# Products with v ahead of a burst's last transposed score, and both bursts of a unit in the order transposed, score, score, transposed

## The chip, the core and the metric

The kernel runs on one core of a Trainium2 chip. The metric is the device time of one execution in microseconds; the time before is the median of three runs. The engines are TensorE (PE; its weight loads are the rows PEld), VectorE (DVE), ScalarE (ACT), GpSimd (POOL) and SyncE (SP), which issues the DMAs. Everything here about the hardware is read from the traces of this kernel.

## What is computed

A block with attention and an MLP side by side, on 2048 rows of 512 features: 32 heads of 16 features, and a hidden layer of 1792.

```python
def _A_ref(x, wqkv, wo):
    qkv = (x @ wqkv).reshape(B, S, 3, H, Dh).transpose(2, 0, 3, 1, 4)
    q, k, v = qkv[0], qkv[1], qkv[2]
    scores = jnp.einsum("bhqd,bhkd->bhqk", q, k) * (Dh ** -0.5)
    p = _softmax(scores, axis=-1)
    o = jnp.einsum("bhqk,bhkd->bhqd", p, v)
    return o.transpose(0, 2, 1, 3).reshape(B, S, D) @ wo

def _B_ref(x, w1, b1, w2, b2):
    h = _gelu(jnp.einsum("bsd,df->bsf", x, w1) + b1)
    return jnp.einsum("bsf,fd->bsd", h, w2) + b2

xn = _layernorm(x)
return x + _A_ref(xn, A_wqkv, A_wo) + _B_ref(xn, B_w1, B_b1, B_w2, B_b2)
```

## The kernel before

**Work.** A prologue (to some 99 us) normalises x, splits it and the first weights into two f16 parts each, and computes the first scores. Then a single stream of *units* carries everything else: attention is cut into 512 units, each with four heads, 512 queries and 128 keys, and the *dense* products (the rest of the projections, both layers of the MLP, the output projection) are put between, some with each unit. A short tail finishes the output projection.

**What a unit does.** For each of its four heads there are three kinds of product:

- *S*, a score (queries by keys, `s_half`, tile pS). VectorE takes its row maximum (L363). It belongs to a unit 19 ahead (`LEAD`), so that the maximum is known in time.
- *T*, a transposed score (keys by queries, `e_half`, tile pT). ScalarE takes its exponential into a tile pe (L410).
- *V*, the product of pe with v (`v_half`, tile pV), in f32. It uses exponentials of one or two units earlier. A row of ones in v gives the sums of the softmax as well.

**Row halves.** Scores contract over 64 rows or fewer. So every product uses one half of the rows of TensorE's array, lower (rows 0 to 63) or upper (64 to 127), and two products in different halves can run side by side. Each product is four instructions, one for each group of 32 columns (`tiled`, L195). A head with an even number works in the lower half, an odd one in the upper half. `v_half` takes two heads' worth of work in a half: keys 0 to 63 with a = 0, keys 64 to 127 with a = 1; its f32 operands make two passes of four instructions.

**A burst.** `unit` (L745) makes two *bursts*, a = 0 and a = 1. Each gives TensorE two T, two S, one V and three or four dense products, in this order of the program:

- a = 0: T1 (upper), S0 (lower), S1 (upper), T0 (lower), then V in the upper half, then dense products in the lower half.
- a = 1: S2 (lower), T3 (upper), S3 (upper), T2 (lower), then V in the lower half, then dense products in the upper half.

So each half has V in one burst of a unit and the dense products in the other. The number of dense products is the group's `pace` (FAST is four in each burst, SLOW three, MEAN three and four by turns). A dense group of 12 or 42 products for each half adds up in one PSUM bank, then ScalarE or VectorE evicts it (`one_more`, L670, issues that after a burst's scores).

**The fence.** V of one burst and V of the next write the same accumulator from different halves, and so do the dense products. They must not overlap. `leave` (L178) lets the last V and the last dense product of a burst raise a semaphore, if the accumulation goes on; a dense group that is finished raises none there. `enter` (L187) sets a goal, and the first product afterwards waits until all these have signalled. In the trace this wait stands on V's first weight load. Everything behind it in TensorE's queue waits too.

**Banks.** S takes turns in three PSUM banks, T in three, a dense group holds one. `hold` (L112) gives a new dense group the bank that T used longest ago; the finished group's bank goes to T (`Group.end`, L550). For the first burst of the 16 units of an accumulation (`new`), V comes after the dense products.

**Who sets the order.** The order on every engine is the order of the program (`manual_schedule`, L840). In the stream of units it is written by hand in `unit`; a planner (`Plan`) orders the prologue alone.

Of the kernel before, what the change touches and what calls it, by code (L numbers as in the profile page):

```python
# [54 lines left out]
def layer_kernel(ctx: ExitStack, tc: tile.TileContext, x, wqkv, wo, w1, b1, w2, b2, out):  # L55
# [51 lines left out]
    def banks(tag):  # L107
        k = free_banks[tag].pop(0)
        free_banks[tag].append(k)
        return bank_tile(k, tag)  # L110

    def hold(tag, other):  # L112
        k = free_banks[tag if free_banks[tag] else other].pop(0)
        return bank_tile(k, tag), (k, other)
# [44 lines left out]
    def given(engine, ns):  # L159
        backlog[engine] += ns  # L160
# [6 lines left out]
    def product(user, *args, **kw):  # L167

        p = nc.tensor.matmul(*args, **kw)  # L169
        if user is None:  # L170
            return
        if goal[0] is not None:
            p._wait_ge(turns, counted[0])
            tc.declare_fence(p.ins, group=goal[0])
            goal[0] = None
        newest[user] = p

    def leave(user, goes_on):  # L178

        p = newest.pop(user, None)  # L180
        if p is not None and goes_on:
            p.then_inc(turns, 1)
            tc.no_tile_sem_insts.add(p.ins.name)
            counted[0] += 1
            left.append(p)

    def enter():  # L187

        if left:
            goal[0] = f"turn{counted[0]}"  # L190
            for p in left:
                tc.add_to_no_dep_group(goal[0], p.ins)
            left.clear()

    def tiled(user, dst, lhs, rhs, start, stop):  # L195

        for j in range(0, P, 32):
            product(user, dst[j:j + 32], lhs[:, j:j + 32], rhs, start=start, stop=stop)
# [11 lines left out]
    def fetch_scale(m):  # L210

        scale_of[m] = nc.scalar.alloc_register(f"sexp{m}")
        nc.scalar.reg_load(scale_of[m], sexp[0:1, m:m + 1].bitcast(I32))
# [152 lines left out]
    def s_half(u, n):  # L366

        s = banks("S")
        s_mm(u, n, s)
        s_max(u, n, s)  # L370

    def s_end(u):

        t, i = divmod(u, 16)
        if i < 15:
            return
        g, qb = divmod(t, NQB)
        mneg = mnegs[t % 2]
        nc.vector.tensor_reduce(mneg[:, :16], mt_of[t].rearrange("p h t k -> p (h t) k"), axis=AX.X, op=ALU.max, negate=True)
        given("dve", 220)  # L380

        def store():

            pt = banks("T")
            for a in range(2):
                nc.tensor.matmul(pt[32 * a:32 * a + 32, :64], mneg[64 * a:64 * a + 64, :],
                                 ident[64 * a:64 * a + 64, 64 * a:64 * a + 64], start=True, stop=True)
            mhl = work.tile([64, 2, 64], F16, name="mhl", bufs=2)
            nc.vector.tensor_scalar_mul(mhl[:, 0], pt[:64, :64], 1.0 / MROW)
            nc.vector.scalar_tensor_tensor(mhl[:, 1], pt[:64, :64], 1.0 / MROW, mhl[:, 0], op0=ALU.mult, op1=ALU.subtract)  # L390
            given("dve", 300)
            for a in range(2):
                nc.sync.dma_start(m_d[t, :, :, 64 * a:64 * a + 64], mhl[32 * a:32 * a + 16])
            for h in range(4):
                m_rows(t, h)

        stores[t] = store

    def e_half(u, n):

        p, a = divmod(n, 2)
        t, kt = divmod(u, 16)
        g, qb = divmod(t, NQB)
        st = banks("T")
        r = slice(64 * a, 64 * a + 64)
        k0 = (kt % 4) * P
        tiled(None, st, kst[g % 2][kt // 4][r, p, k0:k0 + P], qst[g % 2][qb][r, p, :], True, True)
        pe = work.tile([P, QB], F32, name="pe", bufs=12)
        ptiles[u, n] = pe
        nc.scalar.activation(pe, st, AF.Exp, scale=scale_of[g // 2])  # L410
        given("act", 520)

    def v_half(u, a):

        t, kt = divmod(u, 16)
        g, qb = divmod(t, NQB)
        if kt == 0 and a == 0:
            pv_of[t] = hold("V", "S")
        pv = pv_of[t][0]
        r = slice(64 * a, 64 * a + 64)  # L420
        for h in (2, 3, 0, 1):
            c = (4 * g + h) * VW
            product("V", pv[32 * h:32 * h + 32, :], vv[r, kt, c:c + 32], ptiles[u, h][r],
                    start=(kt == 0 and a == 0), stop=(kt == 15 and a == 1))
# [77 lines left out]
    NU = NG * NQB * 16  # L502
# [155 lines left out]
    def ended(at_once=True):  # L658

        if cur[0] is not None and cur[0].over():  # L660
            done, cur[0] = cur[0], None
            ends.append(done.end)
            if at_once:
                settle()
# [5 lines left out]
    def one_more():  # L670

        if ends:
            ends.pop(0)()
        elif extras:
            extras.pop(0)()
# [10 lines left out]
    def dense(gen, side):  # L686

        f = group(gen)
        for _ in range(0 if f is None else f.pace[pos[0] % 2]):
            if not f.usable(side):  # L690
                return
            f.product(side)
# [25 lines left out]
    def spare(gen, side):  # L718

        if extra[0] is None and not spent[0]:  # L720
            f = next(gen, 0)
            spent[0] = f == 0
            extra[0] = Halves(f) if f else None
        if extra[0] is not None:
            extra[0].product(side)
            if extra[0].at == extra[0].n:
                extra[0] = None
# [17 lines left out]
    def unit(gen):  # L745


        u = pos[0]
        e = u - LEAD
        if e > 0 and e % (2 * NQB * 16) == 0 and e < NU:  # L750
            fetch_scale(e // (2 * NQB * 16))
        pos[0] += 1
        for a in range(2):
            for kind, b in ((1, 1), (0, 0), (0, 1), (1, 0)) if a == 0 else ((0, 2), (1, 3), (0, 3), (1, 2)):
                if kind and 0 <= e < NU:
                    e_half(e, b)
                elif not kind and u < NU:
                    s_half(u, b)
                elif not kind and u > NU:
                    spare(gen, b % 2)  # L760
            if e >= 0:
                one_more()
                enter()

                w, r = (e - 2, 1) if a == 0 else (e - 1, 0)
                live = 0 <= w < NU
                new = r == 0 and w % 16 == 0
                if live and not new:
                    v_half(w, r)
                dense(gen, 1 - r)  # L770
                if live and new:
                    v_half(w, r)

                for user, goes_on in (("V", live and not (r == 1 and w % 16 == 15)),
                                      ("D", cur[0] is not None and not cur[0].over())):
                    leave(user, goes_on)
                for k in backlog:
                    backlog[k] = max(0, backlog[k] - HALF)
                if live and r == 1:
                    v_end(w)  # L780
                ended(False)

            if a == 0 and u % 16 == 0 and u // 16 - 1 in stores:
                stores.pop(u // 16 - 1)()
        if u < NU:
            s_end(u)
        tick()
# [9 lines left out]
    with ExitStack() as st1:  # L797
# [252 lines left out]
        for w in (1, 0):  # L1050
# [5 lines left out]
            else:  # L1056
                a = add("POOL", 800, lambda wf=wf, i1=i1: nc.gpsimd.tensor_scalar(tl[wf], tl[wf], i1, 0.0, op0=ALU.mult, op1=ALU.add), [h])
                w_ready[w] = add("POOL", 1100, lambda wf=wf, hi=hi, lo=lo: nc.gpsimd.tensor_tensor(lo, tl[wf], hi, op=ALU.subtract), [a], free=[wf])
        a = add("DVE", 90, lambda: nc.vector.tensor_tensor(sexp[:, 0:1], fac0[:, 0:1], fac0[:, 1:2], op=ALU.mult), [chain])
        a = add("DVE", 90, lambda: nc.vector.tensor_scalar_mul(sexp[:, 0:1], sexp[:, 0:1], DH ** -0.5), [a])  # L1060
# [5 lines left out]
        a = add("DVE", 90, lambda: nc.vector.tensor_tensor(amv[:, 2:3], amv[:, 0:1], amv[:, 1:2], op=ALU.max), v_sum)  # L1066
# [3 lines left out]
        for i in range(2):  # L1070
# [6 lines left out]
            else:  # L1077
                b = add("POOL", 1240, lambda key=key: nc.gpsimd.tensor_scalar(
                    tl[key], tl[key], inv_v[:, 0:1], 0.0, op0=ALU.mult, op1=ALU.add), [h])
# [30 lines left out]
        a = add("DVE", 220, maxima, m_last)  # L1110
# [3 lines left out]
        def turn_m():  # L1114
            tl[mkey] = sb_tile(mkey)
            for k in range(2):
# [3 lines left out]
        a = add("PE", 300, turn_m, [a], take=[mkey])  # L1120
        a = add("DVE", 160, lambda: nc.vector.tensor_scalar_mul(mhl[:, 0], tl[mkey][:64, :64], 1.0 / MROW), [a])
        a = add("DVE", 160, lambda: nc.vector.scalar_tensor_tensor(mhl[:, 1], tl[mkey][:64, :64], 1.0 / MROW, mhl[:, 0],
                                                                   op0=ALU.mult, op1=ALU.subtract), [a], free=[mkey])
# [371 lines left out]
```

## Time and profile before

| | us |
|---|---|
| median of three runs | 1475.2 (1474.68 to 1475.99) |
| the profiled execution | 1476.9 |
| its span, first to last instruction | 1475.1 |
| TensorE busy, at least one row half | 1458.9 |
| VectorE busy | 1356.4 |
| ScalarE busy | 1260.5 |
| GpSimd busy | 662.4 |
| granted TensorE clock | 0.997 |

A row of the timeline is: start, length, engine, line of the kernel, operation, tile written and tiles read, shape, number of instructions run together, and in brackets the idle time before it with what ended it. Lengths of rows with several instructions run from the first start to the last end. The end of a matmul is modelled, and two matmuls in one half overlap at their ends, so the time that a product holds its half is read from start to start. A row with `x8` of a 4-instruction product holds two products. TensorE's products nearly all stand under L169, the helper that records them, so one goes by tiles: pT, pS, pV, pD.

### The profile page before, as it was taken

Reading aid. Unit: us, or ns where it says so; the run is one execution under the profiler, and the core shown is the slowest. Engines: PE = TensorE matmul, PEld = TensorE weight load, DVE = VectorE, ACT = ScalarE, POOL = GpSimd, SP = SyncE. Lnnn points to the kernel's source line nnn. Section 1 sums busy time; section 2 is a strip of 40 time slices with the busy share of each in tenths; the row PEclk is TensorE's granted clock in tenths of the full one; section 3 lists DMA queues with packets and bytes.
Section 4 is the critical chain, followed back from the end, with each engine's and each line's share of the span. In section 5 each row is a group of like instructions: output and inputs, shape, how many; then the busy total and the mean of one; then the engine's idle time right before and its main releaser. Section 6 shows DMA issues by size and latency. Waiting matters only on the chain.

```text
span 1475.1 us, 88125 instructions
## 1 busy us (share of the span) xinstructions
PE 1458.9 (99%) x40158; PEld 817.6 (55%) x40158; DVE 1356.4 (92%) x2305; ACT 1260.5 (85%) x2366; POOL 662.4 (45%) x672
## 2 busy tenths in 40 slices
PE   8999999999999999999999999999999999999998
PEld 4445555565555555555555555555555555555554
DVE  7889999999999999999999999999999999999933
ACT  5868888888999888899988889998889999888884
POOL 3201847563778401287830138783115777121100
PEclk9999999999999999999999999999999999999999
DMA  7732455545224210221113111121112110221432
GB/s 214 225 117 69 151 186 172 169 159 159 78 59 128 66 34 25 70 61 41 45 43 87 30 37 44 51 76 44 44 37 76 55 37 21 57 55 31 142 94 96
DMA packets 112623, 124.83 MB, mean 85 GB/s; under 512 B 22908, under 2 KB 84220, under 8 KB 112248
## 3 DMA queue, kind: packets, MB, share of 16 engines
q1 hardware_dynamic: 112248, 119.18, 27.0%
q8 instruction: 314, 5.14, 1.4%
q14 instruction: 61, 0.50, 0.1%
HBM read 81.66 MB, written 37.34 MB: 81 GB/s over the span
## 4 chain that ended last, share of the span: by engine, by line
PE 95%; ACT 2%; DVE 1%; DMA 1%; issue 0%; SPq 0%; DVEq 0%; ACTq 0%
PE pV L169 29%; PE pD L169 25%; PE pT L169 19%; PE pS L169 19%; PE pT L992 2%; DMA wq<-in_A_wqkv_dram 1%; PE pD L992 1%; DVE mt L363 1%; ACT pe L410 0%; DVE ac L1370 0%; DMA m_d<-mhl 0%; PE pT L962 0%; ACT xs L945 0%; ACT hh L1312 0%; PE pS L1158 0%
## 5 line engine op out<-in xcount | busy, mean ns | idle before, releaser
L363 DVE TENSOR_REDUCE mt<-pS 128x1 f32<-128x512 f32 x2029 | 1278.9, 684 | 54.9 <-PE pS L169 27.0
L410 ACT ACTIVATE pe<-pT 128x512 f32<-128x512 f32 x2048 | 1111.4, 599 | 168.1 <-PE pS L169 79.8
L169 PE MATMUL pV<-pe,vv 64*32 64x512 f32 x8192 | 1074.3, 594 | 0.1
L169 PE MATMUL pT<-qst,kst 64*32 64x512 f16 x8192 | 707.4, 377 | 2.0 <-issue 1.3
L169 PE MATMUL pS<-kst,qst 62*32 62x512 f16 x8116 | 611.1, 378 | 1.2 <-DVE mt L363 1.2
L169 PEld LDWEIGHTS <-qst 62*32 62x32 f16 x8192 | 286.0, 92 | 228.9 <-issue 55.3
L169 PE MATMUL pD<-xb,wc 64*32 64x512 f16 x5376 | 362.1, 377 | 0.0
L169 PEld LDWEIGHTS <-kst 64*32 64x32 f16 x8192 | 276.1, 91 | 154.7 <-issue 62.1
L169 PE MATMUL pD<-w_s,g 64*32 64x512 f16 x5376 | 358.0, 377 | 0.0
L169 PEld LDWEIGHTS pV<-pe,vv 64*32 64x32 f32 x8192 | 182.3, 105 | 89.2 <-PE pV L169 4.2
L169 PE MATMUL pD<-xt,wqk_h 64*32 64x512 f16 x2400 | 158.7, 378 | 0.1
L169 PEld LDWEIGHTS <-wc 64*32 64x32 f16 x5376 | 117.2, 91 | 41.0 <-issue 0.7
L169 PEld LDWEIGHTS <-g 64*32 64x32 f16 x5376 | 114.5, 92 | 39.7 <-issue 0.3
L1337 POOL TENSOR_TENSOR xa<-xa,yt 128x512 f32<-128x512 f32 x16 | 20.5, 1280 | 226.8 <-ACT yt L1335 226.8
L466 POOL TENSOR_TENSOR osb<-osb,rb 128x512 f32<-128x512 f32 x31 | 39.8, 1284 | 165.3 <-DMA rb<-den_d 154.2
L1289 POOL TENSOR_TENSOR t<-hh 128x512 f32<-128x512 f32 x56 | 58.2, 1039 | 84.0 <-ACT hh L1312 83.1
L1291 POOL TENSOR_TENSOR t<-t,hh 128x512 f32<-128x512 f32 x56 | 71.8, 1282 | 4.7
L1284 POOL TENSOR_TENSOR t<-t,hh 128x512 f32<-128x512 f32 x56 | 71.7, 1281 | 4.7
L1286 POOL TENSOR_TENSOR g<-t,g 128x512 f16<-128x512 f32 x56 | 65.2, 1164 | 4.7
L1283 POOL TENSOR_SCALAR t<-t,gs 128x512 f32<-128x512 f32 x56 | 38.8, 693 | 63.3 <-ACT t L1278 63.3
L169 PEld LDWEIGHTS <-wqk_h 64*32 64x32 f16 x2400 | 54.4, 92 | 20.5 <-issue 2.3
L169 PE MATMUL pD<-wo_s,oc 64*32 64x512 f16 x828 | 54.5, 378 | 0.0
(160 smaller groups left out, 873.1 us busy)
## 6 DMA issues: line engine op xcount, KB each, us to landing
wc<-w_d SPq DMA_DIRECT2D x56, 256.0 KB
qk_d<-stg SPq DMA_DIRECT2D x32, 256.0 KB
rb<-den_d SPq DMA_DIRECT2D x124, 64.0 KB
wch<-in_B_w_dram SPq DMA_DIRECT2D x14, 512.0 KB
wch<-in_B_w_dram SPq DMA_DIRECT2D x28, 256.0 KB
w_d<-wsp SPq DMA_DIRECT2D x28, 256.0 KB
kst<-qk_d SPq DMA_DIRECT2D x64, 96.0 KB
qst<-qk_d SPq DMA_DIRECT2D x64, 96.0 KB
```

The lines of the kernel that those rows point to most:

```text
L169: p = nc.tensor.matmul(*args, **kw)
L363: nc.vector.reduce_max(mt_of[t][:, n, qt, kb:kb + 1], s, axis=AX.X)
L410: nc.scalar.activation(pe, st, AF.Exp, scale=scale_of[g // 2])
L466: pooled((1280, lambda: nc.gpsimd.tensor_tensor(osb, osb, rb, op=ALU.mult)), (620, lambda: nc.gpsimd.tensor_scalar(ot[:, 0], osb, 1.0, 0.0 ...
L992: nc.tensor.matmul(tl[key], lhs, rhs, start=c + n == 0, stop=(c, n) == (NC - 1, 2))
L1283: pooled((690, lambda: nc.gpsimd.tensor_scalar(t1, t1, 1.0, gs[:, 1:2], op0=ALU.add, op1=ALU.mult)), (1280, lambda: nc.gpsimd.tensor_tenso ...
L1284: (1280, lambda: nc.gpsimd.tensor_tensor(t1, t1, hh, op=ALU.mult)),
L1286: (1160, lambda: nc.gpsimd.tensor_tensor(g[:, 1, f, :], t1, g[:, 0, f, :], op=ALU.subtract)),
L1289: pooled((1040, lambda: nc.gpsimd.tensor_tensor(t1, hh, hh, op=ALU.mult)), (620, lambda: nc.gpsimd.tensor_scalar(t1, t1, 1.0, 1.0 / GELU_A ...
L1291: (1280, lambda: nc.gpsimd.tensor_tensor(t1, t1, hh, op=ALU.mult)),
L1337: add = lambda: nc.gpsimd.tensor_tensor(xa, xa, yt, op=ALU.add)
```

## The change

The fence and V move ahead of the last of the burst's four T and S products, when V goes on with an accumulation (`early`). In the program the burst is then T, S, S, fence, V, T, dense. In the burst a = 1 the four products are put in another order: T2 (lower), S3 (upper), S2 (lower), T3 (upper), where it was S2, T3, S3, T2. So T0 (a = 0) and T3 (a = 1) come behind V. Where V begins an accumulation, and at the very end, the place of V and of the fence stays. The eviction of a dense group (`one_more`) is still issued after all four products.

```diff
         for a in range(2):
-            for kind, b in ((1, 1), (0, 0), (0, 1), (1, 0)) if a == 0 else ((0, 2), (1, 3), (0, 3), (1, 2)):
+            w, r = (e - 2, 1) if a == 0 else (e - 1, 0)
+            live = 0 <= w < NU
+            new = r == 0 and w % 16 == 0
+            early, placed = live and not new and e < NU, 0
+            for kind, b in ((1, 1), (0, 0), (0, 1), (1, 0)) if a == 0 else ((1, 2), (0, 3), (0, 2), (1, 3)):
                 if kind and 0 <= e < NU:
+                    if placed == 3 and early:
+                        enter()
+                        v_half(w, r)
                     e_half(e, b)
                 elif not kind and u < NU:
                     s_half(u, b)
                 elif not kind and u > NU:
                     spare(gen, b % 2)
+                placed += 1
             if e >= 0:
                 one_more()
-                enter()
-
-                w, r = (e - 2, 1) if a == 0 else (e - 1, 0)
-                live = 0 <= w < NU
-                new = r == 0 and w % 16 == 0
-                if live and not new:
+                if not early:
+                    enter()
+                if live and not new and not early:
                     v_half(w, r)
                 dense(gen, 1 - r)
                 if live and new:
```

In the diff `kind` is 1 for T and 0 for S, and `b` is the head.

## The prediction

> **What bounds the kernel now.** I read the page first, then the instructions that touch the accumulator pV, then the groups of TensorE, then stretches of the timeline.
>
> ```profile
> span 1475.1 us, 88125 instructions
> PE 1458.9 (99%) x40158; PEld 817.6 (55%) x40158; DVE 1356.4 (92%) x2305; ACT 1260.5 (85%) x2366; POOL 662.4 (45%) x672
> ...
> PE 95%; ACT 2%; DVE 1%; DMA 1%; issue 0%; SPq 0%; DVEq 0%; ACTq 0%
> ```
>
> ```profile
> L169 PEld LDWEIGHTS pV<-pe,vv x8192: 102/104/110, 99.2 to 1460.7; 64*32 64x32 f32 x200
> ```
>
> TensorE carries 95% of the chain of waits, but a busy share of 99% doesn't say whether both row halves of its array are busy. The bursts with products with v run from 99.2 to 1460.7 us: 1361.5 us for 512 units, 2.66 us a unit of two bursts, 92% of the span. The change acts only there. How much dense work goes into them:
>
> ```profile
> L169 PE MATMUL pD<-xb,wc 64*32 64x512 f16 x5376 | 362.1, 377 | 0.0
> L169 PE MATMUL pD<-w_s,g 64*32 64x512 f16 x5376 | 358.0, 377 | 0.0
> L169 PE MATMUL pD<-xt,wqk_h 64*32 64x512 f16 x2400 | 158.7, 378 | 0.1
> L169 PE MATMUL pD<-wo_s,oc 64*32 64x512 f16 x828 | 54.5, 378 | 0.0
> ...
> L169 PE MATMUL pD<-wvh,xt 64*32 64x512 f16 x480 | 31.5, 377 | 0.0
> ...
> L169 PE MATMUL pD<-wo_s,xb 64*32 64x512 f16 x336 | 22.6, 378 | 0.0
> ```
>
> Together 14,796 tiles, four to a product: 14796 / 4 / 1024 = 3.61 products a burst. So I treat 39% of the units as having three dense products a burst and 61% as having four. First the timeline of TensorE in a stretch with three (start, length, number of tiles):
>
> ```profile
> 463.27 0.62 PE L169 MATMUL pV<-pe,vv 64*32 64x512 f32 x4
> 463.30 0.61 PE L169 MATMUL pD<-xb,wc 64*32 64x512 f16 x8
> 463.71 0.61 PE L169 MATMUL pV<-pe,vv 64*32 64x512 f32 x4
> 463.73 0.39 PE L169 MATMUL pD<-xb,wc 64*32 64x512 f16 x4
> 463.95 0.39 PE L169 MATMUL pT<-qst,kst 64*32 64x512 f16 x4
> 464.14 0.42 PE L169 MATMUL pS<-kst,qst 62*32 62x512 f16 x8
> 464.36 0.40 PE L169 MATMUL pT<-qst,kst 64*32 64x512 f16 x4
> 464.53 0.63 PE L169 MATMUL pV<-pe,vv 64*32 64x512 f32 x4
> 464.58 0.61 PE L169 MATMUL pD<-xb,wc 64*32 64x512 f16 x8
> ```
>
> This is a burst with V in the lower half (463.27), followed by one with V in the upper half (464.53). An f16 product holds its half for 0.22 us (dense at 463.73, T1 behind it in the same half at 463.95). V comes in two passes 0.44 us apart and holds its half for 0.87: from 463.27 to S0 at 464.14. The lower half then runs S0 at 464.14, T0 at 464.36, dense at 464.58: no hole. The upper half runs T1 at 463.95, S1 0.22 behind it, and V could follow at about 464.38 but starts at 464.53.
>
> **What V waits for.** V's first weight load carries the fence of L187: the last V and the last dense product of the burst before must have signalled. The second pass of 463.71 ended at 463.71 + 0.61 = 464.32, the dense product at 463.73 + 0.39 = 464.12. V starts 0.21 after the later of the two. Three bursts on, a dense group had ended, so the fence waited for V alone:
>
> ```profile
> 465.82 0.62 PE L169 MATMUL pV<-pe,vv 64*32 64x512 f32 x4
> ...
> 466.26 0.61 PE L169 MATMUL pV<-pe,vv 64*32 64x512 f32 x4
> ...
> 466.91 0.40 PE L169 MATMUL pT<-qst,kst 64*32 64x512 f16 x4
> 466.96 0.63 PE L169 MATMUL pV<-pe,vv 64*32 64x512 f32 x4
> 467.13 0.39 PE L169 MATMUL pD<-xb,wc 64*32 64x512 f16 x4
> ```
>
> There V starts 0.09 after the end of the second pass (466.87), 0.12 sooner, although T0 stood just as long before (0.65 after the second pass in both). So the fence waited for the signal of a dense product that had ended 0.2 us before V: TensorE's signals seem to leave in the order of the program, each behind those ahead of it. ScalarE shows the same:
>
> ```profile
> 1197.66 0.61 PE L169 MATMUL pV<-pe,vv 64*32 64x512 f32 x4
> 1197.72 0.39 PE L169 MATMUL pT<-qst,kst 64*32 64x512 f16 x4
> ```
>
> ```profile
> 1198.61 0.60 ACT L410 ACTIVATE pe<-pT 128x512 f32<-128x512 f32 x1 [0.55 <-PE pS L169]
> ```
>
> T ended at 1198.11, V's second pass, ahead of it in the program, at 1198.27; the exponential of T starts at 1198.61 after 0.55 us of idle time.
>
> The Trainium skill (TensorE: Matmul & The Clock Gate, section The mechanism) says that matmuls both start and end strictly in the order of the program. The trace agrees on the ends, by the two waits just read. On the starts it does not: the dense products of 463.30 stand behind V's second pass in the program and start 0.41 us ahead of it.
>
> Now the stretch with four dense products:
>
> ```profile
> 471.19 0.59 PE L169 MATMUL pV<-pe,vv 64*32 64x512 f32 x1
> ...
> 471.62 0.59 PE L169 MATMUL pV<-pe,vv 64*32 64x512 f32 x2
> ...
> 472.49 0.62 PE L169 MATMUL pV<-pe,vv 64*32 64x512 f32 x4
> ...
> 473.82 0.59 PE L169 MATMUL pV<-pe,vv 64*32 64x512 f32 x1
> ```
>
> ```profile
> 472.47 0.13 PEld L169 LDWEIGHTS pV<-pe,vv 64*32 64x32 f32 x5
> ```
>
> The unit takes 473.82 - 471.19 = 2.63. A half's own work is V 0.87 + eight products (S, T, four dense, T, S) x 0.22 = 2.63: packed full. The fence opens at 472.47, 0.85 after the second pass, when S0 and T0 have just covered it. With three dense products the half's work is 2.41, but the unit takes 465.82 - 463.27 = 2.55, set by the fence in each burst. By shares: 0.39 x 2.55 + 0.61 x 2.63 = 2.60; the measured 2.66 leaves 0.06 a unit, 31 us in all, for other waits.
>
> **The change, part by part.**
>
> (1) The transposed score that was third or fourth in the burst (T0, or T3 in the other burst) now stands behind V's waiting weight load. Behind the load also stand the dense products and the next burst, as before; ScalarE waits for this T, and the group's eviction waits for the dense products. T was what filled the half while the fence was shut. Now that half has V's 0.87 and one S, is free at 1.09 after V's start, and waits for the fence.
>
> (2) When does it open? Second pass 0.44 after V's start, then 0.82 (463.71 to 464.53) with three dense products or 0.85 with four. New in it is T's own signal, which now lies between V's and the dense product's. The trace doesn't show that place. Bounds: 0, and the 0.12 that the signal of three dense products costs; I take 0.06, since T has fewer instructions than these. Then 0.05 for handing V over (V 464.53 to dense 464.58). T starts 0.44 + 0.82 + 0.06 + 0.05 = 1.37 after V's start with three, 1.40 with four.
>
> (3) A unit of one half then is that start plus T, the dense products, T and S: 1.37 + 6 x 0.22 = 2.69 with three, 1.40 + 7 x 0.22 = 2.94 with four. By shares 2.84; times 512 it is 1454 us, against 1361.5 now. The 0.06 of part (2) bounds it to 1423 and 1485.
>
> (4) The T moved behind V signals only after V's second pass. Its exponential follows V's start by 0.44 + 0.61 + some 0.15 of signals, about 1.2, and takes 0.6 (row above), so its bank is free about 1.8 after V's start. Three banks in turn cover that. When a dense group ends, though, the new one takes the oldest T bank, and the second T of the next burst gets the bank of its forerunner and waits from about 1.4 to 1.8. There are some 115 groups (5376 / 96 = 56 of the first dense layer, 16 of the second, the rest projections): at most 115 x 0.4 = 46 us, at least 0. With the 31 us of other waits that may stay or be swallowed by the new holes, this term lies between 0 and 77; I take 20, nearer the low end because a half that idles 0.3 us a unit absorbs much.
>
> (5) The new order in the second burst (T2, S3, S2, T3) leaves each half with the same products. It shifts a score or a T by one product, 0.22 us at most either way a unit. VectorE and ScalarE cover it:
>
> ```profile
> 857.77 1.27 DVE L363 TENSOR_REDUCE mt<-pS 128x1 f32<-128x512 f32 x2
> ```
>
> ```profile
> L363 DVE TENSOR_REDUCE mt<-pS 128x1 f32<-128x512 f32 x2029 | 1278.9, 684 | 54.9 <-PE pS L169 27.0
> L410 ACT ACTIVATE pe<-pT 128x512 f32<-128x512 f32 x2048 | 1111.4, 599 | 168.1 <-PE pS L169 79.8
> ```
>
> Two maxima back to back are 1.27 - 0.68 = 0.59 apart, 2.36 for a unit's four; that leaves 0.5 of 2.84. If VectorE were the bound, the 0.22 would cost up to 113 us. I count 0. No DMA is moved, and nothing passes SP's or POOL's queue.
>
> (6) V itself may start earlier than T0 let it (464.38 against 464.53); that gives nothing while the fence opens later than both.
>
> Sum: 1454 + 20 - 1361 = +113 us. The profiled execution took 1476.9 us, span 1475.1, and the runs' median is 1475.2; the sum on the execution gives 1590, on the median **1588**.
>
> **The rivals.**
>
> A. Only the cover is lost: T's signal costs nothing and the new holes swallow all other waits. For it: holes of 0.3 us a unit. Against it: signals that queue behind one another at 464.53. 1423 - 1361 = +62: 1537.
>
> B. Faster. V is held not by signals but by its place behind T0; ahead of T0 it starts when its half is free, and T0 still fills the other half. For it: V starts 0.17 after T0 (464.36 to 464.53) with its half free since 464.38. Against it: at 466.91 the same T0 is followed by V in 0.05. The gain would be 0.15 a burst in the 39% with three dense products, 400 x 0.15 = 60 us at most; VectorE's 2.36 a unit leaves room for it. I take 35: 1440. It decides if T0 starts within 0.7 of V's second pass, as it does now.
>
> C. No difference: VectorE sets the pace (92% busy) and TensorE's new holes fall into its waits. Against it: VectorE needs 2.36 of 2.66. 1475.
>
> D. T0 must wait until V's second pass has started, 0.44 later. Against it: the dense products at 463.30. 0.44 x 512 = 225 on top: 1813. That is what the Trainium skill's rule on starts (same section) would make of it.
>
> **How the numbers follow.** Forecast 0.61 (its own range 1545 to 1645), A 0.17, B 0.13, C 0.08, D 0.01. A measurement of this kernel can tell about 0.2%, 3 us, from no change. C gives 0.04 to the same, 0.03 to slower and 0.01 to faster. Slower is 0.61 + 0.17 + 0.01 + 0.03 = 0.82, faster 0.14, same 0.04. The range goes from C, 1474, up to 1650, the forecast with three quarters of the waits in (4) and T's signal at 0.1; B, D and what little of the others lies beyond are left out, under 2 in 10.
>
> **What would show it.** Right: the starts of V in a stretch with four dense products lie 1.4 to 1.5 apart instead of 1.31; the T behind V starts about 0.05 after the fence opens, some 0.9 after the second pass, with its half idle before it; ScalarE's wait for pT grows, VectorE's share falls to about 86%. Wrong: T0 starting 0.65 after the second pass as now, or V's spacing unchanged with three dense products; then the fence is not what holds the queue, and B or C is left.

## The result and the profile after

| | before | after |
|---|---|---|
| median of the runs, us | 1474.9 | 1631.5 |
| ratio to before | | 1.1057 (95% interval 1.1043 to 1.1072) |
| span of the profiled execution, us | 1475.1 | 1629.0 |
| stream of V, first to last weight load, us | 1361.5 | 1515.5 |

The change costs 157 us, and 154 of them lie in the stream of units. The page of the changed kernel (busy time and share of each engine, the rows of VectorE's maxima and ScalarE's exponentials with their idle time ahead), and the row of V's weight loads with their first and last start:

```profile
span 1629.0 us, 88631 instructions
...
PE 1609.9 (99%) x40158; PEld 914.1 (56%) x40158; DVE 1384.4 (85%) x2305; ACT 1273.9 (78%) x2366; POOL 662.0 (41%) x672
...
L363 DVE TENSOR_REDUCE mt<-pS 128x1 f32<-128x512 f32 x2029 | 1304.3, 685 | 171.9 <-PE pT L169 108.7
L410 ACT ACTIVATE pe<-pT 128x512 f32<-128x512 f32 x2048 | 1124.2, 597 | 308.6 <-PE pT L169 262.6
```

```profile
L169 PEld LDWEIGHTS pV<-pe,vv x8192: 102/106/110, 99.1 to 1614.6; 64*32 64x32 f32 x200
```

TensorE's own row still says 99%: one half idles while the other works, and the busy share can't show it. VectorE and ScalarE show it. Idle time ahead of the maxima rose from 54.9 to 171.9 us, ahead of the exponentials from 168.1 to 308.6, and nearly all the new waits are for pT. The same stretch as before, with three dense products a burst, on TensorE's timeline:

```profile
789.43 0.62 PE L169 MATMUL pV<-pe,vv 64*32 64x512 f32 x4
789.45 0.40 PE L169 MATMUL pT<-qst,kst 64*32 64x512 f16 x4
789.67 0.39 PE L169 MATMUL pD<-xb,wc 64*32 64x512 f16 x4
789.87 0.60 PE L169 MATMUL pV<-pe,vv 64*32 64x512 f32 x3
...
790.30 0.40 PE L169 MATMUL pS<-kst,qst 62*32 62x512 f16 x4
790.32 0.39 PE L169 MATMUL pT<-qst,kst 64*32 64x512 f16 x4
790.53 0.39 PE L169 MATMUL pS<-kst,qst 62*32 62x512 f16 x4
790.76 0.62 PE L169 MATMUL pV<-pe,vv 64*32 64x512 f32 x4
790.78 0.40 PE L169 MATMUL pT<-qst,kst 64*32 64x512 f16 x4
791.01 0.39 PE L169 MATMUL pD<-xb,wc 64*32 64x512 f16 x4
...
792.10 0.62 PE L169 MATMUL pV<-pe,vv 64*32 64x512 f32 x4
```

```profile
790.75 0.13 PEld L169 LDWEIGHTS pV<-pe,vv 64*32 64x32 f32 x5 [0.16 <-PE pD L169]
```

The upper half has V at 789.43 and 789.87 and one product at 790.30. It is free at 790.52 and then stands empty until T at 790.78. T came 0.03 after V's weight load, 0.91 after the second pass, 1.35 after V's start. In the kernel before, T0 ran 0.65 after the second pass, in that hole. The trace also records when signals arrive: V's at 790.521, that of the T of 789.45 (ended by 789.85) at 790.581, the dense product's at 790.706, and V's load follows at 790.75. In bursts 60 to 960, V's load comes within 60 ns of the last signal it waits for in 91% of the bursts, in the kernel before in 92%: the fence sets V's start in both. The unit takes 792.10 - 789.43 = 2.67. With four dense products:

```profile
779.11 0.62 PE L169 MATMUL pV<-pe,vv 64*32 64x512 f32 x4
779.13 0.40 PE L169 MATMUL pT<-qst,kst 64*32 64x512 f16 x4
...
780.66 0.60 PE L169 MATMUL pV<-pe,vv 64*32 64x512 f32 x4
780.73 0.60 PE L169 MATMUL pD<-xb,wc 64*32 64x512 f16 x8
...
782.03 0.62 PE L169 MATMUL pV<-pe,vv 64*32 64x512 f32 x4
```

The unit takes 2.92. By the same shares (0.39 and 0.61) these undisturbed units make 2.82, times 512 1445 us. The stream takes 1515.5, so 70 us are other waits, against 31 before. Where a dense group ends they can be seen (timeline of TensorE, its weight loads and ScalarE):

```profile
774.21 0.74 PE L169 MATMUL pV<-pe,vv 64*32 64x512 f32 x4
...
774.39 0.40 PE L169 MATMUL pT<-qst,kst 64*32 64x512 f16 x4
...
774.66 0.71 PE L169 MATMUL pV<-pe,vv 64*32 64x512 f32 x4
774.88 0.83 PE L169 MATMUL pD<-xb,wc 64*32 64x512 f16 x12
...
775.53 0.40 PE L169 MATMUL pD<-xb,wc 64*32 64x512 f16 x4
...
775.58 0.60 ACT L410 ACTIVATE pe<-pT 128x512 f32<-128x512 f32 x1 [0.26 <-PE pT L169]
...
775.99 0.12 PEld L169 LDWEIGHTS pV<-pe,vv 64*32 64x32 f32 x4
...
776.18 0.61 PE L169 MATMUL pV<-pe,vv 64*32 64x512 f32 x4
...
776.23 0.40 PE L169 MATMUL pT<-qst,kst 64*32 64x512 f16 x4
```

T at 774.39 ended at 774.79. Its exponential starts only at 775.58, after V's second pass has ended (774.66 + 0.71 = 775.37). It ends at 776.18, and the T that gets its bank starts at 776.23. What kept V back here began in the same way a burst earlier (same timeline):

```profile
772.89 0.40 PE L169 MATMUL pT<-qst,kst 64*32 64x512 f16 x4
...
773.48 0.61 PE L169 MATMUL pV<-pe,vv 64*32 64x512 f32 x4
...
773.75 1.08 ACT L410 ACTIVATE pe<-pT 128x512 f32<-128x512 f32 x2
```

The T of 772.89, behind V too, ended at 773.29. Its exponential, the second of the two in the last row, starts at 774.23, after V's second pass (773.48 + 0.61 = 774.09), and ends at 774.83. The new dense group has this T's bank, so its first product starts at 774.88, 0.67 after V. The burst's last dense product ends at 775.93, and only then, at 775.99, comes the next V's load. V's spacing is 776.18 - 774.21 = 1.97 instead of 1.46.

To size this, the start of every V was taken from the traces, the ends of dense groups found in the trace of before (a burst with dense products after which V's signal alone opens the fence; there are 114, while an expectation below goes by 134), and the three spacings after each end set against the others:

| kernel | mean spacing away from ends, us | three spacings after an end, beyond three others, us |
|---|---|---|
| before | 1.320 | 0.09 |
| after | 1.432 | 0.44 |
| V ahead in the first burst only | 1.415 | 0.37 |
| V ahead, old order | 1.420 | 0.30 |
| score behind V | 1.428 | 0.04 |
| after, two fences | 1.392 | 0.55 |
| score behind V, two fences | 1.383 | 0.18 |

Of the 154 us some (1.432 - 1.320) x 1023 = 115 lie away from the ends and (0.44 - 0.09) x 114 = 40 at them. The late bank shows in the same count: in the changed kernel the first dense product behind V starts on average 0.57 after V in the burst after an end and 0.22 elsewhere, with a score behind V 0.22 and 0.19.

### The profile page after: what moved, and what is told of

It is laid out like the page before. It is cut to its first block, busy times and chain, and to the rows that moved or that the text cites. A ratio compares the mean times of both kernels' runs of the same rounds, so it can differ in the third digit from the quotient of the medians.

```text
span 1629.0 us, 88631 instructions
## 1 busy us (share of the span) xinstructions
PE 1609.9 (99%) x40158; PEld 914.1 (56%) x40158; DVE 1384.4 (85%) x2305; ACT 1273.9 (78%) x2366; POOL 662.0 (41%) x672
## 4 chain that ended last, share of the span: by engine, by line
PE 95%; ACT 2%; DMA 1%; DVE 1%; issue 0%; SPq 0%; DVEq 0%; ACTq 0%
PE pV L169 30%; PE pD L169 27%; PE pS L169 24%; PE pT L169 12%; PE pT L997 1%; DMA wq<-in_A_wqkv_dram 1%; ACT pe L410 1%; PE pD L997 0%; DMA qk_d<-stg 0%; DVE ac L1375 0%; DMA kst<-qk_d 0%; ACT xs L950 0%; DVE mt L363 0%; PE pT L386 0%; ACT wqk_h L886 0%
## 5 line engine op out<-in xcount | busy, mean ns | idle before, releaser
L363 DVE TENSOR_REDUCE mt<-pS 128x1 f32<-128x512 f32 x2029 | 1304.3, 685 | 171.9 <-PE pT L169 108.7
L410 ACT ACTIVATE pe<-pT 128x512 f32<-128x512 f32 x2048 | 1124.2, 597 | 308.6 <-PE pT L169 262.6
L169 PE MATMUL pT<-qst,kst 64*32 64x512 f16 x8192 | 764.7, 381 | 3.2 <-ACT pe L410 3.0
L169 PE MATMUL pS<-kst,qst 62*32 62x512 f16 x8116 | 733.7, 379 | 1.4 <-DVE mt L363 1.2
L169 PEld LDWEIGHTS <-qst 62*32 62x32 f16 x8192 | 294.0, 90 | 179.6 <-issue 82.4
L169 PEld LDWEIGHTS pV<-pe,vv 64*32 64x32 f32 x8192 | 214.6, 105 | 159.1 <-PE pD L169 69.1
L169 PEld LDWEIGHTS <-kst 64*32 64x32 f16 x8192 | 237.9, 91 | 88.9 <-issue 28.7
L169 PEld LDWEIGHTS <-wc 64*32 64x32 f16 x5376 | 143.3, 92 | 88.9 <-issue 19.2
L169 PEld LDWEIGHTS <-g 64*32 64x32 f16 x5376 | 142.2, 93 | 75.8 <-issue 6.3
L169 PEld LDWEIGHTS <-wqk_h 64*32 64x32 f16 x2400 | 64.0, 93 | 33.1 <-issue 4.6
```

The lines of the kernel that those rows point to most:

```text
L363: nc.vector.reduce_max(mt_of[t][:, n, qt, kb:kb + 1], s, axis=AX.X)
```

## The experiments

Theory F is the prediction's: the product behind V no longer covers the wait at the fence (with V's, T's and the dense product's signals in the order of the program), and T's late signal makes ScalarE late. All ratios are to the kernel before on the same chip.

**The new order alone.**

```diff
-            for kind, b in ((1, 1), (0, 0), (0, 1), (1, 0)) if a == 0 else ((0, 2), (1, 3), (0, 3), (1, 2)):
+            for kind, b in ((1, 1), (0, 0), (0, 1), (1, 0)) if a == 0 else ((1, 2), (0, 3), (0, 2), (1, 3)):
```

> The kernel before with only the new order T, S, S, T in the second burst; the fence and V stay behind all four. Theory F (the T behind V no longer covers the wait at the fence, and its signal comes behind V's): nothing in that is touched, so the time stays within 5 us of 1475. Rival O (the new order is what costs, by when scores and transposed scores reach VectorE and ScalarE): a large part of the 157 us is there, 1540 or more.

Measured: 1471.2 us, ratio 0.9965 (0.9947 to 0.9984). The order doesn't cost, it gains 5 us; rival O falls. With the new order, the whole loss and a little more hangs on the place of V.

**V ahead in the first burst of a unit only.**

```diff
-            early, placed = live and not new and e < NU, 0
+            early, placed = live and not new and e < NU and a == 0, 0
```

> The changed kernel with the fence and V ahead of the last T in the first burst of a unit only (a = 0). Theory F: the lower half alone loses its cover, but the two halves are tied by the fence, so its unit sets the pace. No T's signal lies between the second burst's V and dense product, so its T starts 1.31 (three dense products) or 1.34 (four) after V, the unit takes 2.63 or 2.88, 1425 us for the 512, 64 more than before; half of the waits at the ends of dense groups, some 20, come on top: 1545 to 1570. Rival O: the new order is still in it, so it stays near 1631. Rival P (each V ahead costs for itself, whichever half): half of the 157, 1553 - which doesn't tell it from F by the total, but then V's spacing is long after one burst and as before after the other.

Measured: 1605.1 us, ratio 1.0872 (1.0853 to 1.0890). That is 82% of the loss for one burst of the two, so the losses of the two bursts don't add. O and P are out by the total, though the sign named for P is there: the next V starts on average 1.61 after a burst with V ahead (1.38 in the kernel before) and 1.30 after the other (1.28; starts of V in bursts 60 to 960). So nearly the whole loss comes right after the V that was moved. F's direction holds, but its number was 35 us too low; the table shows 0.37 at each end of a group, most of what both bursts give.

**Two fences instead of one.** V waits for V alone, dense products for dense products alone.

```diff
-    counted, left, newest, goal = [0], [], {}, [None]
+    counted, left, newest, goal = {"V": 0, "D": 0}, {"V": [], "D": []}, {}, {"V": None, "D": None}
...
-        if goal[0] is not None:
-            p._wait_ge(turns, counted[0])
+        if goal[user] is not None:
+            p._wait_ge(turns[user], counted[user])
```

In the changed kernel:

> The changed kernel with two semaphores instead of one: V waits only for the V of the burst before, a dense product only for the dense product of the burst before. Theory F: V's wait no longer holds the dense product's signal and the T's ahead of it, the fence opens some 0.15 to 0.2 earlier, T starts 1.19 after V's start, the unit takes 2.51 or 2.73, 2.64 by shares: 85 to 95 us less than the changed kernel, about 1545. Rival Q (T waits for V itself, its weight loads or its passes, not for the signals): 1631 within 10.

Measured: 1603.7 us, ratio 1.0858 (1.0839 to 1.0876): 28 us less, a third of what F said. In the kernel before:

> The kernel before with the same two semaphores. Theory F: with four dense products a burst the halves are packed and nothing is gained; with three the fence sets the unit (2.55) and it falls to about 2.43: 0.39 x 512 x 0.12 = 24 us less, 1451. Rival Q: 1475 within 5.

Measured: 1464.2 us, ratio 0.9920 (0.9904 to 0.9937): 12 us less, half of what F said, and not nothing as Q had it. So the signals do hold the fence, in both kernels, but behind it stands something else. One candidate is the T banks, at the ends of groups; the next kernel takes T away from behind V.

**A score behind V instead of a transposed score.**

```diff
-            for kind, b in ((1, 1), (0, 0), (0, 1), (1, 0)) if a == 0 else ((1, 2), (0, 3), (0, 2), (1, 3)):
+            for kind, b in ((1, 1), (1, 0), (0, 1), (0, 0)) if a == 0 else ((1, 2), (1, 3), (0, 2), (0, 3)):
+                if placed == 3 and early:
+                    enter()
+                    v_half(w, r)
                 if kind and 0 <= e < NU:
-                    if placed == 3 and early:
-                        enter()
-                        v_half(w, r)
                     e_half(e, b)
```

> The changed kernel with a score S, not a transposed score, behind V: T1, T0, S1, V, S0 in the first burst and T2, T3, S2, V, S3 in the second. Theory F: the half still has nothing to run while the fence is shut (93 us, as worked out for T), but both T signal ahead of V, so ScalarE is not late and the waits for T's banks go: 1560 to 1590. Late is then one S in each burst, which VectorE can take with its three banks. Rival T (the cost hangs on a transposed score being behind V, by its exponential alone): back to 1475 to 1500. Rival V (whatever stands behind V costs the same): 1631 within 10.

Measured: 1581.0 us, ratio 1.0710 (1.0685 to 1.0734), inside F's 1560 to 1590. Away from the ends nothing changes (1.428 against 1.432), so the lost cover costs the same whatever stands behind V. At the ends 0.44 falls to 0.04: with both transposed scores ahead of V, their late signal is gone. T and V are both out as the only reason.

**The score behind V, with two fences.**

> The kernel with a score behind V (1581 us), and with two fences. The changed kernel gained only 28 us from two fences, not 85 to 95. Theory F: there the T's bank took over where the fence let go; with a score behind V no T is late, so the fence's earlier opening (by the dense product's signal and one more, 0.18 to 0.22 a burst) shows nearly in full: 75 to 95 us less, 1486 to 1506. Rival Q (what stands behind V waits mostly for V itself, and the separate fences are worth some 28 us wherever they are put): 1550 to 1560.

Measured: 1549.1 us, ratio 1.0490 (1.0473 to 1.0508): 32 us less, as Q said and not as F. The T banks were not what kept two fences from paying. Its timeline, with four dense products a burst, shows what did:

```profile
739.91 0.63 PE L169 MATMUL pV<-pe,vv 64*32 64x512 f32 x4
...
740.34 0.63 PE L169 MATMUL pV<-pe,vv 64*32 64x512 f32 x4
...
740.77 0.60 PE L169 MATMUL pT<-qst,kst 64*32 64x512 f16 x8
...
741.14 0.45 PE L169 MATMUL pS<-kst,qst 62*32 62x512 f16 x8
741.14 0.11 PEld L169 LDWEIGHTS pV<-pe,vv 64*32 64x32 f32 x1
741.15 0.10 PEld L169 LDWEIGHTS <-qst 62*32 62x32 f16 x3
...
741.36 0.59 PE L169 MATMUL pV<-pe,vv 64*32 64x512 f32 x1
```

The second pass ends at 740.97 and its signal is recorded at 741.014, yet V's weight load comes at 741.14, 0.13 after the signal where 0.04 is usual, in the moment when the last score of V's own half starts (V follows it by 0.22, at 741.36). The score behind V, in the other half, has its weights loaded right after that, at 741.15. So even with the fence open a product behind V waits until V's half has come to its last product ahead of V. With three dense products a burst that half is early: a unit takes 2.51 where little else disturbs it, F's 2.51 (the median is 2.56); with four it takes 2.80, not 2.73 (starts of V in this trace).

A count over the traces bears this out. Of bursts 60 to 960 there are 872 in which V waits for the V before it. In the changed kernel with two fences, V's load comes more than 60 ns after that signal in 424 of them, and in 408 of these it comes just as a score or a transposed score starts, which V follows by 0.20 to 0.23, the time that one such product holds its half. Here these are 271; in the changed kernel with one fence 56 of 900. What keeps V's half back so long is not settled by the count, and no run took that wait away.

**V ahead with the old order.** The diff of the first experiment, undone in the changed kernel: T2, which comes behind V in the second burst, is then in V's own half.

> The changed kernel with the old order in the second burst (S2, T3, S3, then V, then T2): the product behind V is then in V's own half, and the dense products of the upper half stand behind it. Theory F: T2 cannot run before V's second pass has left, some 0.9 after V's start, the dense products come through the queue only 0.4 to 0.5 after V's start, end that much later and hold the next fence shut by 0.2 to 0.4 longer than in the changed kernel, once in a unit: 100 to 200 us more, 1730 to 1830. Rival O (the new order brought part of the loss): less than 1631.

Measured: 1604.1 us, ratio 1.0866 (1.0848 to 1.0884), 27 us less than the changed kernel. F's range misses by 126 us. The timeline shows why (V at 514.69 is the one in question, w_s,g the dense products behind T2):

```profile
514.69 0.63 PE L169 MATMUL pV<-pe,vv 64*32 64x512 f32 x4
514.73 0.61 PE L169 MATMUL pD<-w_s,g 64*32 64x512 f16 x8
515.14 0.61 PE L169 MATMUL pV<-pe,vv 64*32 64x512 f32 x4
515.17 0.39 PE L169 MATMUL pD<-w_s,g 64*32 64x512 f16 x4
515.39 0.58 PE L169 MATMUL pT<-qst,kst 64*32 64x512 f16 x8
515.61 0.58 PE L169 MATMUL pS<-kst,qst 62*32 62x512 f16 x8
516.17 0.63 PE L169 MATMUL pV<-pe,vv 64*32 64x512 f32 x4
```

The dense products start 0.04 after V, ahead of T2, which waits for its half until 515.57 (0.43 after the second pass). Here a product that waits for its half lets products of the other half past, whereas V's load in the experiment before held back the score behind it; what makes the difference is not shown. In this burst the other half had T3 and S3 as cover, so that burst loses no cover. But T2's signal leaves late and ahead of the dense products'. V's is recorded at 515.795, T2's at 515.998, and that of the dense products, which ended by 515.56, at 516.124. The next V comes at 516.17, 1.03 after the second pass, which fits a gain of only 27 us.

**A fourth bank for T, taken from S.**

```diff
-    free_banks = {"S": [0, 1, 2], "T": [3, 4, 5], "D": [6], "V": [7]}
+    free_banks = {"S": [0, 1], "T": [2, 3, 4, 5], "D": [6], "V": [7]}
```

In the changed kernel:

> The changed kernel with one PSUM bank moved from the scores S (three to two) to the transposed scores T (three to four). Theory F, with its size corrected by the traces (of the 157 us some 115 come in bursts away from the ends of dense groups, where T waits at the fence, and some 43 in the three bursts after each of 134 ends, where T or a dense product waits for a bank whose exponential is late because T's signal comes behind V's): the second part goes, 1575 to 1595, as far as VectorE gets by with two banks (the next run says what that costs). Rival B (the waits at the ends are those for evictions or for VectorE, not for T's banks): 1631 or more, and the difference to the next run stays 157.

Measured: 1701.2 us, ratio 1.1522 (1.1497 to 1.1548). In the kernel before:

> The kernel before with the same two banks for S and four for T: the control. Theory F: its T signals come early, so a fourth bank gains at most the 7 us that the ends of groups cost here, and two banks for S cost something: 1470 to 1500. The changed kernel with four T should lie 95 to 115 us above it, not 157.

Measured: 1634.6 us, ratio 1.1068 (1.1040 to 1.1095). The control failed: two banks are far too few for the scores, and the kernel before loses 159 us. Its row of maxima shows VectorE waiting for scores:

```profile
L363 DVE TENSOR_REDUCE mt<-pS 128x1 f32<-128x512 f32 x2029 | 1288.4, 685 | 194.0 <-PE pS L169 176.2
```

The difference of the two is 67 us, neither F's 95 to 115 nor 157, and another wait has come into both: in the changed kernel, too, 207.9 us of VectorE's idle time are put down to pS. The pair says nothing on T's banks.

**Both edits that gained, on the kernel before.** The new order and two fences, V behind all four products.

> The kernel before with the new order in the second burst and with two fences, V behind all four products: the two edits that gained alone (0.35% and 0.8%). If they add up, 1458 to 1462; if the new order's gain was time that the separate fences already save, 1464.

Measured: 1455.8 us, ratio 0.9857 (0.9836 to 0.9879), the fastest of all, 20 us under the kernel before. The two add up (5 and 12 us); the few us on top lie within the intervals.

## Why the prediction was right, and where it was off

The forecast was 1588 (+113), the measured time is 1631.5 (+157): the right sign and the right mechanism, and a size too small by 44 us.

1. *T behind V waits at the fence, and its half stands empty.* Seen as said: T starts 0.03 after V's weight load. By the starts of all T behind V in bursts 60 to 960 of the trace, some 630 of 900 come within 60 ns of that load; another 175 come within 0.1 us after the end of an exponential, which frees a bank.
2. *When the fence opens.* Forecast 1.37 and 1.40 after V's start, T's signal taken as 0.06. Measured 1.35 with three dense products. The load came 790.75 - 789.87 = 0.88 after the second pass, 0.06 more than the 0.82 before, and T's signal is recorded 0.060 after V's (790.521 and 790.581). The prediction reads such late signals as ends in the order of the program. That goes further than the trace: by its modelled end this T was done at 789.85, before V's second pass (to 790.47), and it is the signals that keep the order.
3. *The units.* Forecast 2.69 and 2.94, measured 2.67 and 2.92; 1454 us forecast for the stream without other waits, 1445 measured.
4. *Other waits.* This is the term that was mis-sized: 20 us taken, bounds 0 and 77, 70 measured. The cause was the one named, T's late signal and a bank freed late after a group's end; the score behind V shows it alone. It came to 0.44 at each of 114 ends, some 50 us, above the bound of 46 (0.4 at 115 ends). The forecast had the next burst's second T waiting for a bank; the trace shows the new group's first product waiting, and with it the fence. The wrong step was to let the new holes absorb the waits: apart from the ends, 20 us are left of the 70, as many as the 31 - 11 = 20 before. The holes lie ahead of T, and a dense product that waits for a bank comes after T; that this is why they absorb nothing is argued, not shown.
5. *The new order.* Counted at 0; alone it gains 5 us.
6. *V could start earlier than T0 let it.* Nothing came of it, as forecast.

A (only the cover is lost, 1537) falls with the ends of groups and with the 0.06 of T's signal. B (faster) falls at T's start, 0.91 after the second pass instead of its limit of 0.7. C falls: VectorE's share went from 92% to 85%. D falls: T at 789.45 runs 0.42 ahead of V's second pass, and the rule on starts in the Trainium skill (TensorE: Matmul & The Clock Gate, section The mechanism), which D rests on, doesn't hold for products in different row halves in this trace.

What the prediction had not seen is the second wait behind the fence, V's own half. In the changed kernel the fence hides it. With two fences V's signal opens the fence earlier, but V's load then comes at its own half's pace in 408 of 872 bursts, and the gain was 28 and 32 us, not 75 and more. At the ends of groups the waits grew as well (0.44 to 0.55 and 0.04 to 0.18), 12 and 16 us. What sets the pace of V's half away from the ends stays open.

## What to carry to other kernels

In a queue that is worked through in order, the instruction that waits for a semaphore should stand behind all work that can run in the meantime: what is moved behind it leaves its unit empty until the wait ends, however short it is itself. Before moving a product ahead, ask which of the products that it passes was filling the other unit, and whose signals now leave behind its own. A fence that stood for two accumulators cost 12 to 32 us more here than two fences, and a busy share of 99% doesn't show a half-empty array.

## What the runs showed that was not expected

- Signals of TensorE left in the order of the program, each some time behind the one ahead (790.521, 790.581 and 790.706 for V, T and the dense product): with T's in between, the fence opened 0.06 later (0.88 against 0.82).
- A product waiting for its own row half lets later products of the other half past (dense products at 514.73 ahead of T2 at 515.57); behind a weight load waiting at the fence nothing came past in the rows read (a half free at 790.52, its T at 790.78).
- Moving one of the scores' three banks to the transposed scores costs 159 us in the kernel before.
